# Several scheduling edits at once in an attention-and-expand kernel: opening order, value sums, value lag, and the start of the next product

## The chip, the cores and the metric

The kernel runs on one core of one Trainium2 chip. The metric is the device time of that core in microseconds, as the median of several executions. Experiments are compared with runs of the kernel before, made on the same chip in the same rounds.

## The reference

Hash attention feeds a gated expand and a contraction. Shapes: batch 4, 8 heads, 768 tokens, head width 64; the second half has 3072 tokens, width 512 and inner width 2048.

```python
q_bits = (einsum('bhsd,dk->bhsk', q, proj) > 0)      # 6 hash bits per token, the same for k
mask   = q_bucket[:, :, :, None] == k_bucket[:, :, None, :]
scores = where(mask, q @ k.T / sqrt(64), -1e9)
attn   = softmax(scores) ; x = attn @ v               # (B*S, H*D) = 3072 x 512
h = x @ w_in                                          # 512 -> 2048
s = sin(alpha * h)
out = (h + s * s / (alpha + 1e-9)) @ w_out            # 2048 -> 512
```

## The kernel before

The unit is a pair of heads: 16 pairs, four per batch. A pair takes 12 steps (2 heads x 6 key blocks). A step is two score matmuls, one exponential on ScalarE, and, some steps later, six value matmuls ("weigh"). After the first pair of each batch the batch before is expanded: 16 chunks F of 8 matmuls, sine, square and a close on VectorE. Its contraction (96 matmuls of 512 columns) is then mixed into the following pairs, two per step, by `fill`. Of the eight PSUM banks, six form three score slots of two; bank 6 and bank 7 take values and contraction sums.

```python
def weigh(step):                                     # values of one step
    if kb == 0:                                      # sum of all values, for empty buckets
        nc.tensor.matmul(out=regions..., lhsT=empty,
            rhs=vsum[:, hh, :]...broadcast [128, SB, D+1], start=True, stop=False)
    for qb in range(SB):
        nc.tensor.matmul(out=regions[...65 columns], lhsT=e[...], rhs=vaug[:, hh, kb, :],
                         start=False, ...)
    if kb == SB - 1:
        finish_head(i, hh, acc, xn)                  # VectorE: reciprocal, product

def attend(i, at_step, lag=2):
    accs = [banks[:, 6, :], banks[:, 7 if i <= NPAIR else 6, :]]
    for n in range(2 * SB):
        ...                                          # scores, exponential
        at_step(n)                                   # pieces of later pairs, loads, fill(2.0)
        while len(behind) > lag + (behind[0][2] == 0):
            weigh(behind.pop(0))

def prepare_on_pe(i):                                # pairs 0 to 5: hash bits on PE
    ...                                              # transposes on VectorE
    ps, held = slot(hold=True)                       # a score slot, held to the end
    hash_into(ps[:, 0], turned)                      # then pick into ps[:, 1]
    ...
    for h in range(2):
        if h == 1 and i == 0: give_back(held); ps, held = slot(hold=True)
        ...                                          # 12 transposes, two copies to aug
# [cut: prepare_by_dma for pairs 6 to 15 turns q and k by DMA transposes]

# expand:   h = banks[:, 6:8, :] if F % 4 == 2 else slot()[0]
# contract: o = banks[:, 7, :]; after 16 matmuls VectorE copies o to osb and it is stored
# at_step:  if n == 4: load(i + 3);  if n == 4 and 0 < i <= 4: weigh_in(...)  # one weight piece
```

The 16 weight pieces are 512 KB each, loaded as float32 and cast to bfloat16 on POOL; `weigh_in` issues one load and the cast of an earlier piece.

The softmax here doesn't subtract the row's maximum and nothing guards it: scores larger than these inputs give would overflow.

## Time and profile before

| | before |
|---|---|
| median | 334.79 us (3 runs, 334.19 to 336.34) |
| span of the profiled execution | 332.0 us |
| first exponential | 15.74 us |
| first expand begins, ends | 66.69, 87.69 us |
| last expand begins | 284.50 us |

The boundaries are start times of matmuls and exponentials in the trace. First the page's busy times (PE is TensorE's matmuls, PEld the loading of their stationary operand, DVE VectorE, ACT ScalarE, POOL GpSimd), then groups of it (busy us, mean ns of one, idle before and its releaser):

```profile
PE 305.9 (92%) x3016; PEld 184.5 (56%) x3041; DVE 182.2 (55%) x302; ACT 243.8 (73%) x299; POOL 93.8 (28%) x175
```

```profile
L367 ACT ACTIVATE e<-banks 128x768 bf16<-128x768 f32 x192 | 150.4, 810 | 42.4 <-PE banks L360 34.0
...
L333 PE MATMUL banks<-vsum,empty 128*128 128x390 bf16 x32 | 10.6, 331 | 0.0
```

The waits of PE (engine, line, what it waited for: total us, times, longest):

```profile
PE banks L427 <- DVE osb L435: 5.4, 15, 1.0
PE banks L427 <- DVE g L381: 5.2, 4, 1.9
PE banks L196 <- POOL w_hash L146: 4.4, 1, 4.4
PE banks L360 <- ACT e L367: 1.4, 5, 0.4
...
PE banks L427 <- POOL w_out_bf L175: 0.4, 1, 0.4
```

L427 is the contraction: it waits for the copy of its finished block (osb), and at its start for the expand's close (g) that still reads bank 7. L196 is the first hash. A busy PE of 92% includes pipeline tails; streaming times are smaller, so the prediction below counts them by hand.

Busy time by stretch (length, then busy us of PE, PEld, DVE, ACT, POOL; granted clock as a share of the full one; busy share of the DMA engines; GB/s). The first is attention alone, the second the first expand, the third a mixed stretch:

```profile
15.74:66.69 50.95, 48.91 (x812) 34.19 (x810) 31.56 (x66) 44.11 (x60) 25.45 (x48) 1.00 0.50 144
66.69:87.69 21.00, 21.00 (x145) 12.79 (x142) 18.24 (x24) 20.39 (x24) 9.23 (x9) 1.00 0.95 272
...
163.63:217.43 53.80, 50.38 (x534) 29.41 (x541) 25.02 (x48) 40.90 (x51) 11.25 (x21) 1.00 0.60 141
```

And four exponentials in a row, from the timeline (start, us, engine):

```profile
15.74 2.90 ACT L367 ACTIVATE e<-banks 128x768 bf16<-128x768 f32 x4
```

### The profile page before, as it was taken

Reading aid. Unit: us, or ns where it says so; the run is one execution under the profiler, and the core shown is the slowest. Engines: PE = TensorE matmul, PEld = TensorE weight load, DVE = VectorE, ACT = ScalarE, POOL = GpSimd, SP = SyncE. Lnnn points to the kernel's source line nnn. Section 1 sums busy time; section 2 is a strip of 40 time slices with the busy share of each in tenths; the row PEclk is TensorE's granted clock in tenths of the full one; section 3 lists DMA queues with packets and bytes.
Section 4 is the critical chain, followed back from the end, with each engine's and each line's share of the span. In section 5 each row is a group of like instructions: output and inputs, shape, how many; then the busy total and the mean of one; then the engine's idle time right before and its main releaser. Section 6 shows DMA issues by size and latency. Waiting matters only on the chain.

```text
span 332.0 us, 7598 instructions
## 1 busy us (share of the span) xinstructions
PE 305.9 (92%) x3016; PEld 184.5 (56%) x3041; DVE 182.2 (55%) x302; ACT 243.8 (73%) x299; POOL 93.8 (28%) x175
## 2 busy tenths in 40 slices
PE   4799999999889999999899999999899998998995
PEld 4566766666445555566455555566455554564442
DVE  3456566679943443559943443559943212499311
ACT  1287988999976777889987777889987776499000
POOL 2990256515779335235000235130000000000000
PEclk9699999999999999999999999999999999999999
DMA  7902767699874868963013958870015220200031
GB/s 240 331 2 51 206 210 231 169 204 330 299 256 82 222 88 231 218 137 118 0 42 60 237 116 211 216 114 0 3 38 77 85 55 16 72 2 0 11 117 64
DMA packets 68763, 42.86 MB, mean 129 GB/s; under 512 B 46728, under 2 KB 63608, under 8 KB 68728
## 3 DMA queue, kind: packets, MB, share of 16 engines
q1 hardware_dynamic: 68464, 42.37, 48.2%
q8 instruction: 24, 0.39, 0.5%
q14 instruction: 11, 0.09, 0.1%
q10 hardware_dynamic: 264, 0.01, 0.0%
HBM read 28.01 MB, written 7.27 MB: 106 GB/s over the span
## 4 chain that ended last, share of the span: by engine, by line
PE 77%; DMA 8%; DVE 6%; ACT 4%; issue 2%; SPq 2%; POOL 1%; ACTq 0%; POOLq 0%; DVEq 0%
PE banks L427 24%; PE banks L393 18%; PE banks L360 16%; PE banks L340 9%; PE banks L196 4%; DVE osb L435 3%; PE banks L251 3%; DMA w_1468<-in_moe_w_in_dram 3%; ACT e L367 2%; DMA w_1596<-in_moe_w_out_dram 2%; DMA proj_97<-in_proj_dram 2%; PE banks L333 2%; DMA w_1532<-in_moe_w_out_dram 1%; DVE g L381 1%; DMA ka<-kn 1%
## 5 line engine op out<-in xcount | busy, mean ns | idle before, releaser
L367 ACT ACTIVATE e<-banks 128x768 bf16<-128x768 f32 x192 | 150.4, 810 | 42.4 <-PE banks L360 34.0
L427 PE MATMUL banks<-w_out_bf,g 128*128 128x512 bf16 x359 | 98.9, 378 | 13.3 <-DVE osb L435 5.4
L360 PE MATMUL banks<-qa,ka 76*128 76x384 bf16 x384 | 93.1, 325 | 2.0 <-ACT e L367 1.4
L393 PE MATMUL banks<-xt,w_in_bf 128*128 128x384 bf16 x512 | 84.3, 326 | 0.0
L340 PEld LDWEIGHTS <-e 128*128 128x128 bf16 x1152 | 54.4, 97 | 30.4 <-issue 2.1
L393 PEld LDWEIGHTS <-w_in_bf 128*128 128x128 bf16 x512 | 49.7, 98 | 32.5
L427 PEld LDWEIGHTS <-g 128*128 128x128 bf16 x384 | 36.5, 97 | 48.4 <-issue 17.1
L402 ACT ACTIVATE s<-banks,alpha_sb 128x768 bf16<-128x768 f32 x64 | 57.1, 892 | 7.2 <-PE banks L393 5.9
L340 PE MATMUL banks<-vaug,e 128*128 128x65 bf16 x1152 | 60.6, 193 | 0.2 <-ACT e L367 0.2
L435 DVE COPY osb<-banks 128x512 f32<-128x512 f32 x24 | 16.6, 691 | 43.6 <-PE banks L427 43.6
L360 PEld LDWEIGHTS <-ka 76*128 76x128 bf16 x384 | 28.6, 98 | 11.9 <-issue 3.4
L315 DVE RECIPROCAL rden<-banks 128x6 f32<-128x6 f32 x32 | 6.1, 190 | 45.7 <-PE banks L340 45.7
L213 POOL TENSOR_TENSOR vacc<-vacc,vaug 128x130 f32<-128x130 f32 x48 | 20.3, 422 | 3.8
L281 DVE TENSOR_SCALAR bits<-banks,side 128x192 bf16<-128x192 f32 x20 | 7.4, 413 | 22.1 <-ACT e L367 11.5
L196 PE MATMUL banks<-qt,w_hash 128*32 128x192 f32 x128 | 14.3, 344 | 4.6 <-POOL w_hash L146 4.4
L316 DVE TENSOR_TENSOR xn<-banks,rden 128x384 bf16<-128x384 f32 x32 | 17.8, 558 | 1.1
L196 PE MATMUL banks<-kt,w_hash 128*32 128x192 f32 x128 | 14.3, 344 | 0.0
L196 PEld LDWEIGHTS banks<-qt,w_hash 128*32 128x32 f32 x128 | 6.5, 112 | 10.3 <-POOL w_hash L146 4.7
L251 PE MATMUL banks<-ident,nat 128*76 128x128 bf16 x144 | 11.1, 234 | 0.7 <-DVE nat L240 0.7
L251 PEld LDWEIGHTS <-nat 128*76 128x76 bf16 x144 | 10.3, 126 | 2.2 <-POOL vacc L210 0.8
L333 PE MATMUL banks<-vsum,empty 128*128 128x390 bf16 x32 | 10.6, 331 | 0.0
L255 ACT COPY ka<-banks 76x768 bf16<-76x768 bf16 x2 | 1.6, 794 | 12.0 <-PE banks L251 12.0
(269 smaller groups left out, 275.7 us busy)
## 6 DMA issues: line engine op xcount, KB each, us to landing
out_dram<-osb SPq DMA_DIRECT2D x24, 256.0 KB
rows<-bits SPq DMA_DIRECT2D x40, 24.0 KB
w_603<-in_moe_w_in_dram SPq DMA_DIRECT2D x1, 512.0 KB
w_823<-in_moe_w_in_dram SPq DMA_DIRECT2D x1, 512.0 KB
w_1048<-in_moe_w_in_dram SPq DMA_DIRECT2D x1, 512.0 KB
w_1270<-in_moe_w_in_dram SPq DMA_DIRECT2D x1, 512.0 KB
w_1421<-in_moe_w_in_dram SPq DMA_DIRECT2D x1, 512.0 KB
w_1436<-in_moe_w_in_dram SPq DMA_DIRECT2D x1, 512.0 KB
```

Of the source, the lines that this page charges most:

```text
L196: nc.tensor.matmul(out=ps[32 * j:32 * j + 32, 0:SB * 32].rearrange("p (s c) -> p s c", s=SB), lhsT=w_hash[:, blk].rearrange("p l a -> p (l ...
L213: nc.gpsimd.tensor_tensor(out=dst, in0=vacc[:, sb % 2], in1=vaug[:, :, sb], op=ALU.add)
L251: nc.tensor.transpose(out[:, s * 128:(s + 1) * 128], nat[:, s, 2 * t + h], ident)
L316: nc.vector.tensor_tensor(out=xn[:, :, hh, :], in0=cols[:, :, 0:D], in1=rden.unsqueeze(2).to_broadcast([128, SB, D]), op=ALU.mult,)
L333: nc.tensor.matmul(out=regions.rearrange("p (s e) -> p s e", e=D + 1), lhsT=empty, rhs=vsum[:, hh, :].unsqueeze(1).to_broadcast([128, SB, ...
L340: nc.tensor.matmul(out=regions[:, qb * (D + 1):(qb + 1) * (D + 1)], lhsT=e[:, qb * 128:(qb + 1) * 128], rhs=vaug[:, hh, kb, :], start=Fals ...
L360: nc.tensor.matmul(out=sc[:, half, 0:HALF], lhsT=ka[0:KA, hh, kb * 128:(kb + 1) * 128], rhs=qa[0:KA, hh, half * HALF:(half + 1) * HALF], s ...
L367: nc.scalar.activation(out=e.rearrange("p (h c) -> p h c", h=2), in_=sc[:, :, 0:HALF], func=AF.Exp, scale=SCALE,)
L393: nc.tensor.matmul(out=h[:, half, 0:HALF], lhsT=w_in_bf[:, p, F * 128:(F + 1) * 128], rhs=xt[b][:, p, half * HALF:(half + 1) * HALF], star ...
L402: nc.scalar.activation(out=s.rearrange("p (h c) -> p h c", h=2), in_=h[:, :, 0:HALF], func=AF.Sin, scale=alpha_sb[:, F:F + 1],)
L427: nc.tensor.matmul(out=o, lhsT=g[:, F, sub * 128:(sub + 1) * 128], rhs=w_out_bf[:, F, :], start=(F == 0), stop=(F == NF - 1),)
L435: nc.vector.tensor_copy(out=osb, in_=o)
```

## The change

Its intent is to take waits and work from PE: an earlier opening, score slots held for less time, value sums on VectorE for pairs 6 to 15, values three steps behind, a pause after a finished output block, and a contraction that begins inside the expand's last chunk. The diff, cut to its core:

```diff
+        nc.scalar.dma_start(out=proj_sb, in_=proj)            # one plain DMA, first
-            nc.scalar.dma_start(out=proj4[:, blk, :], in_=proj[...].to_broadcast([4, 32, NB]))
# w_hash copied half by VectorE, half by POOL; alpha prepared in the opening; 44 warm-up matmuls for 32
# prepare_on_pe: q and k turned in two pieces; hash and pick in bank 6 for i > 1
+        if i > 1: ps = banks[:, 6, :]
         for h in range(2):
-            if h == 1 and i == 0:
+            if held is not None:
                 give_back(held)
-                ps, held = slot(hold=True)
+            ps, held = slot(hold=True)
# prepare_by_dma: base = the value sums of a pair, one 130-column matmul, copied to SBUF
# finish_head, i >= 6:  total = acc + base  on VectorE, then reciprocal and product
-        if kb == 0:
+        if kb == 0 and not apart:                             # apart = i >= ON_PE
-    def attend(i, at_step, lag=2):
+    def attend(i, at_step, lag=3):
-            while len(behind) > lag + (behind[0][2] == 0):
+            while len(behind) > lag:
# expand
+            at_chunk(F, g)                # last chunk: queue the contraction and fill(4.0, 4)
-            h = banks[:, 6:8, :] if F % 4 == 2 else slot()[0]
+            h = banks[:, 6:8, :] if F in (3, 7, 11) else slot()[0]
# straight after the expand fill(8.0, 8); before, two steps' scores came first
# fill: at most three a step, and none in the step after a finished block ("rest")
# the last output block goes out in two column halves
-            at = [(i - 2, 6 + late), (i - 2, 10 + late // 2), (i - 1, 0), (i - 1, 2), (i - 1, 4), (i - 1, 6)]
+            at = [(i - 2, n) for n in (4, 7, 11)] + [(i - 1, n) for n in (1, 2, 3, 5, 6, 6, 8)]
-                if n == 4 and i + 3 < n_pairs:
+                if n == 6 and i + 3 < n_pairs:
                     load(i + 3)
-                if n == 4 and 0 < i <= NPAIR:
+                if n == 7 and 0 < i <= NPAIR:
                     weigh_in(1 if i < NPAIR else 0)
```

More of the change, by code (lines that the diff above doesn't have):

```diff
@@ L47 @@
     KA = D + 2 * NB
+    ON_PE = 6
     SCALE = 1.0 / (D ** 0.5)
@@ L95, in load @@
                 loaded[i, name] = t
-    proj4 = const.tile([128, 2, NB], FP32, name="proj4")
+    proj_sb = const.tile([D, NB], FP32, name="proj_sb")
     w_hash = const.tile([128, 2, 8, 4], FP32, name="w_hash")
@@ L118, in hash_constants @@
         nc.vector.memset(empty, EMPTY)
-        for blk in range(2):
-            nc.scalar.dma_start(
-                out=proj4[:, blk, :],
-                in_=proj[32 * blk:32 * blk + 32, :].unsqueeze(0).to_broadcast([4, 32, NB]),
-            )
         nc.vector.memset(w_hash, 0.0)
@@ L145, in hash_constants, with invert_alpha @@
         for a in range(4):
-            nc.gpsimd.tensor_copy(
-                out=w_hash[32 * a:32 * a + 32, :, 0:NB, a], in_=proj4[32 * a:32 * a + 32])
+            for blk, engine in ((0, nc.vector), (1, nc.gpsimd)):
+                engine.tensor_copy(
+                    out=w_hash[32 * a:32 * a + 32, blk, 0:NB, a],
+                    in_=proj_sb[32 * blk:32 * blk + 32, :])
     def load_alpha():
-        nc.sync.dma_start(out=alpha_raw, in_=moe_alpha.rearrange("(F p) -> F p", p=128))
+        nc.scalar.dma_start(out=alpha_raw, in_=moe_alpha.rearrange("(F p) -> F p", p=128))
+    def invert_alpha():
         nc.vector.tensor_copy(out=ident32, in_=ident[0:NF, 0:NF])
-    def invert_alpha():
         nc.tensor.transpose(banks[:, 7, 512 - NF:512], alpha_raw, ident32)
@@ L179, with turn_blocks @@
     operands = {}
-    def turn_blocks(i):
-        q2, k2 = loaded.pop((i, "q")), loaded.pop((i, "k"))
-        turned = []
-        for name, src in (("q", q2), ("k", k2)):
-            t = hash_pool.tile([128, 2, SB, 2, 32], FP32, name=f"{name}t")
-            nc.vector.transpose(
-                out=t.rearrange("p h s b c -> p (h s b c)"),
-                in_=src.rearrange("p h s d -> p (h s d)"),
-            )
-            turned.append(t)
-        return q2, k2, turned
+    def turn_blocks(name, src):
+        t = hash_pool.tile([128, 2, SB, 2, 32], FP32, name=f"{name}t")
+        nc.vector.transpose(
+            out=t.rearrange("p h s b c -> p (h s b c)"),
+            in_=src.rearrange("p h s d -> p (h s d)"),
+        )
+        return t
     def hash_into(ps, turned):
-        for j in range(4):
-            for blk in range(2):
+        for blk in range(2):
+            for j in range(4):
                 nc.tensor.matmul(
@@ L216, in prepare_on_pe @@
     def prepare_on_pe(i):
-        q2, k2, turned = turn_blocks(i)
+        q2, k2 = loaded.pop((i, "q")), loaded.pop((i, "k"))
+        turned = [turn_blocks("q", q2)]
         nat = hash_pool.tile([128, SB, 4, KA], BF16, name="nat")
@@ L224, in prepare_on_pe @@
         yield
-        ps, held = slot(hold=True)
-        hash_into(ps[:, 0], turned)
+        turned.append(turn_blocks("k", k2))
+        yield
+        held = None
+        if i > 1:
+            ps = banks[:, 6, :]
+        else:
+            ps, held = slot(hold=True)
+            ps = ps[:, 0, :]
+        hash_into(ps, turned)
         bits = hash_pool.tile([128, SB, 32], BF16, name="bit")
         nc.vector.tensor_scalar(
-            out=bits.rearrange("p s c -> p (s c)"), in0=ps[:, 0, 0:SB * 32],
+            out=bits.rearrange("p s c -> p (s c)"), in0=ps[:, 0:SB * 32],
             scalar1=bound[:, 0:1], scalar2=None, op0=ALU.is_gt,
@@ L232, in prepare_on_pe @@
         yield
-        picked = ps[:, 1, 0:SB * 8 * NB].rearrange("p (s m) -> p s m", s=SB)
+        picked = ps[:, SB * 32:SB * (32 + 8 * NB)].rearrange("p (s m) -> p s m", s=SB)
         for s in range(SB):
@@ L244, in prepare_on_pe @@
         for h in range(2):
-            if h == 1 and i == 0:
+            if held is not None:
                 give_back(held)
-                ps, held = slot(hold=True)
+            ps, held = slot(hold=True)
             for t in range(2):
@@ L251, in prepare_on_pe @@
                     nc.tensor.transpose(out[:, s * 128:(s + 1) * 128], nat[:, s, 2 * t + h], ident)
-            for t in range(2):
-                out = ps[0:KA, t, 0:HALF].bitcast(BF16)
-                if i == 0 and t == 1:
+                if (i, h, t) == (0, 0, 1):
                     nc.scalar.copy(out=aug[t][0:KA, h, :], in_=out)
@@ L257, in prepare_on_pe @@
                     nc.vector.tensor_copy(out=aug[t][0:KA, h, :], in_=out)
-            yield
+                yield
+        values = take_values(i)
+        operands[i] = (*aug, *values)
+        yield
         give_back(held)
-        operands[i] = (*aug, *take_values(i))
     def prepare_by_dma(i):
-        q2, k2, turned = turn_blocks(i)
+        vaug, vsum = take_values(i)
+        yield
+        q2, k2 = loaded.pop((i, "q")), loaded.pop((i, "k"))
+        turned = [turn_blocks("q", q2), turn_blocks("k", k2)]
         nats = []
@@ L290, in prepare_by_dma @@
             )
+        base = v_pool.tile([128, 2, D + 1], FP32, name="base")
+        room = ps[:, 1, 0:2 * (D + 1)]
+        nc.tensor.matmul(
+            out=room, lhsT=empty, rhs=vsum.rearrange("p h e -> p (h e)"), start=True, stop=True)
+        nc.vector.tensor_copy(out=base.rearrange("p h e -> p (h e)"), in_=room)
         yield
@@ L303, in prepare_by_dma @@
                 )
-        yield
-        operands[i] = (*aug, *take_values(i))
+        operands[i] = (*aug, vaug, vsum, base)
     xt = {}
@@ L314, in finish_head @@
         cols = acc[:, 0:SB * (D + 1)].rearrange("p (s e) -> p s e", e=D + 1)
+        if i >= ON_PE:
+            total = x_pool.tile([128, SB, D + 1], FP32, name="total")
+            nc.vector.tensor_tensor(
+                out=total, in0=cols,
+                in1=operands[i][4][:, hh].unsqueeze(1).to_broadcast([128, SB, D + 1]), op=ALU.add,
+            )
+            cols = total
         nc.vector.reciprocal(out=rden, in_=cols[:, :, D])
@@ L329, in weigh @@
         i, hh, kb, e, acc, xn = step
-        _, _, vaug, vsum = operands[i]
+        vaug, vsum = operands[i][2:4]
         regions = acc[:, 0:SB * (D + 1)]
-        if kb == 0:
+        apart = i >= ON_PE
+        if kb == 0 and not apart:
             nc.tensor.matmul(
@@ L343, in weigh @@
                 rhs=vaug[:, hh, kb, :],
-                start=False, stop=(kb == SB - 1 and qb == SB - 1),
+                start=(apart and kb == 0 and qb == 0), stop=(kb == SB - 1 and qb == SB - 1),
             )
@@ L352, in attend @@
             xt[b] = xt_pool.tile([128, NPAIR, S], BF16, name="xt")
-        qa, ka, vaug, vsum = operands[i]
+        qa, ka = operands[i][0:2]
         accs = [banks[:, 6, :], banks[:, 7 if i <= NPAIR else 6, :]]
@@ L372, in attend, with expand @@
             at_step(n)
-            while len(behind) > lag + (behind[0][2] == 0):
+            while len(behind) > lag:
                 weigh(behind.pop(0))
-    def expand(b, at_step):
+    def expand(b, at_chunk):
         g = g_pool.tile([128, NF, S], BF16, name="g")
@@ L411, in expand @@
             close(F, s2, h)
-            at_step(F)
-        return g
     rows_of = [out[b * S:(b + 1) * S, :].rearrange("(p s) d -> p s d", s=SB) for b in range(B)]
@@ L420, in contract @@
         last = b == B - 1
-        order = [(sub, F) for sub in range(SB) for F in range(NF)]
+        order = [(sub, F, 0, DMODEL) for sub in range(SB) for F in range(NF)]
         if last:
-            order[:2 * NF] = [(sub, F) for part in (range(12), range(12, NF))
+            order[:2 * NF] = [(sub, F, 0, DMODEL) for part in (range(12), range(12, NF))
                               for sub in range(2) for F in part]
-        for sub, F in order:
-            o = banks[:, 7 - (sub % 2 if last else 0), :]
+            order[-NF:] = [(SB - 1, F, c, c + DMODEL // 2) for c in (0, DMODEL // 2)
+                           for F in range(NF)]
+        for sub, F, c0, c1 in order:
+            o = banks[:, 7 - ((sub + (c0 > 0)) % 2 if last else 0), c0:c1]
             nc.tensor.matmul(
@@ L429, in contract @@
                 lhsT=g[:, F, sub * 128:(sub + 1) * 128],
-                rhs=w_out_bf[:, F, :],
+                rhs=w_out_bf[:, F, c0:c1],
                 start=(F == 0), stop=(F == NF - 1),
@@ L434, in contract @@
                 osb = o_pool.tile([128, DMODEL], FP32, name="osb")
-                nc.vector.tensor_copy(out=osb, in_=o)
-                nc.sync.dma_start(out=rows_of[b][:, sub, :], in_=osb)
+                nc.vector.tensor_copy(out=osb[:, c0:c1], in_=o)
+                nc.sync.dma_start(out=rows_of[b][:, sub, c0:c1], in_=osb[:, c0:c1])
             yield F == NF - 1
@@ L442, with fill @@
     owed = 0.0
-    def fill(rate):
-        nonlocal owed
+    rest = False
+    def fill(rate, most=3):
+        nonlocal owed, rest
         owed += rate
-        while owed >= 1.0 and todo:
+        if rest:
+            rest = False
+            return
+        while owed >= 1.0 and todo and most:
             owed -= 1.0
+            most -= 1
             done = next(todo[0], None)
@@ L452, in fill @@
             if done:
+                rest = True
                 break
     def drain():
-        nonlocal owed
+        nonlocal owed, rest
         while todo:
             fill(1.0)
-        owed = 0.0
+        owed, rest = 0.0, False
     IN_ATTEND = 2.0
     n_pairs = len(pairs)
-    ON_PE = 6
     parts = {}
@@ L468 @@
         if i == 1:
-            at = [None, (0, 3), (0, 4), (0, 5), (0, 7), (0, 9)]
+            at = [(0, n) for n in (1, 2, 4, 5, 7, 8, 8, 10)]
         elif i < ON_PE:
-            late = 2 if i == 2 else 0
-            at = [(i - 2, 6 + late), (i - 2, 10 + late // 2), (i - 1, 0), (i - 1, 2), (i - 1, 4), (i - 1, 6)]
-        else:
-            at = [(i - 2, 6), (i - 2, 10), (i - 2, 11), (i - 1, 3), (i - 1, 5), (i - 1, 6)]
-        for part in at[1:] if i == 1 else at:
+            at = [(i - 2, n) for n in (4, 7, 11)] + [(i - 1, n) for n in (1, 2, 3, 5, 6, 6, 8)]
+        else:
+            at = [(i - 2, n) for n in (3, 6, 10, 11)] + [(i - 1, n) for n in (1, 3)]
+        for part in at:
             parts.setdefault(part, []).append(i)
@@ L480 @@
         hash_constants()
+        load_alpha()
         load(0, "kv")
         load(1, "qk")
-        for _ in range(32):
+        for _ in range(44):
             nc.tensor.matmul(out=banks[:, 7, 0:128], lhsT=empty, rhs=empty, start=True, stop=True)
-        for _ in prepare_on_pe(0):
-            pass
         load(1, "v")
         load(2)
+        first = prepare_on_pe(0)
+        for _ in range(3):
+            next(first)
+        invert_alpha()
+        for _ in range(3):
+            next(first)
         under_way = {1: prepare_on_pe(1)}
-        next(under_way[1])
+        for _ in range(2):
+            next(under_way[1])
+        for _ in first:
+            pass
         weights = iter(range(16))
@@ L499, in weigh_in, with at_chunk @@
                 cast_w(*held_w.popleft(), nc.gpsimd)
+        done = 0
+        def at_chunk(F, g):
+            nonlocal done
+            if done == 0:
+                weigh_in(2)
+            if F == NF - 1:
+                todo.append(contract(done, g))
+                done += 1
+                fill(4.0, 4)
         for i in range(n_pairs):
@@ L508, in at_step @@
                     next(under_way[p], None)
-                if (i, n) == (1, 4):
-                    load_alpha()
-                if (i, n) == (3, 4):
-                    invert_alpha()
-                if n == 4 and i + 3 < n_pairs:
+                if n == 6 and i + 3 < n_pairs:
                     load(i + 3)
-                if n == 4 and 0 < i <= NPAIR:
+                if n == 7 and 0 < i <= NPAIR:
                     weigh_in(1 if i < NPAIR else 0)
-                if n == 0 and i % NPAIR == 1:
-                    return
                 fill(IN_ATTEND)
@@ L523 @@
                 drain()
-                g = expand(b - 1, lambda F: weigh_in(2) if b == 1 else None)
-                todo.append(contract(b - 1, g))
-                owed = 8.0
+                expand(b - 1, at_chunk)
+                fill(8.0, 8)
         while behind:
@@ L529 @@
         drain()
-        todo.append(contract(B - 1, expand(B - 1, lambda F: None)))
+        expand(B - 1, at_chunk)
         drain()
```

## The prediction

> **What bounds it now.** TensorE. The page gives PE 92% busy, but that counts pipeline tails. From the timeline, streaming rates are 0.1625 us per 384-column matmul (120 in 19.50 us), 0.2155 us per 512-column one, 0.03 us per 65-column value matmul (six between starts 0.18 us apart), 0.81 us per hash group of 16, 0.33 us per pick group, 0.67 us per 12 transposes. Summed over the counts this is about 291 us of the 332 us span. The Trainium skill, "TensorE: Matmul & The Clock Gate" (Part 1), says N/2.4 GHz + 2.5 ns; the 0.1625 us agrees. So about 41 us are gaps, tails and the cold start.
>
> Stages by windows: opening 0 to 14.7; five attention pairs alone 14.7 to 68 (53 us; ScalarE's 60 exponentials of 0.81 us are a floor of 48.6 us); four expands of 21 us, in which PE, ACT and DVE are all near 100%; three stretches of attention with the contraction mixed in (54, 54, 46 us; per step PE 0.94 us against ACT 0.81, so PE-bound); last contraction 21 us.
>
> **What the change does, costed.**
> 1. Opening. The waits view shows the first hash waiting 4.4 us for w_hash, whose projection DMA landed at 8.0 us. One plain DMA issued first should land near 3 us, so the hash waits for the transpose of k (ends 7.1) instead: 2 us. PE idle shrinks from 4.4 us to about 2, so the clock may stay up (0.57 was granted in 8 to 16 us; hash group 1.6 us there, 0.81 later). First scores from 14.8 to about 12: -2.5 to -3.
> 2. Attention alone: hash no longer holds a score slot, lag three: ACT idle there is about 3 to 4 us, I give back -1.5.
> 3. Start of contraction. PE waited 1.1, 1.1, 1.0, 1.9 us for bank 7, which chunk 14 of the expand held. Now chunks 3, 7, 11 hold it, and four matmuls run inside the last chunk: about -4.5.
> 4. Pause after a finished output block: waits for the osb copy, 5.4 us in 15 pieces (up to 1.0): -4.
> 5. Value sums: 20 matmuls of 390 columns (0.165 us) go, ten of 130 columns (about 0.06) come: -2.7 on PE. DVE gets 20 adds of about 0.56 us and ten small copies, off the path since DVE is near 50% there. But both heads use bank 6, and the next head's values now come one step (about 0.76 us) after the last, while the add frees the bank after about 0.8: 0.1 to 0.2 us stall a head, +2 to +3.
> 6. Last output in halves: -0.4.
> 7. First contraction reaches the last w_out chunk sooner; its DMAs are already back to back (about 0.95 share, cast ended 95.5): +1.
>
> Sum: about -14 to -16 us.
>
> **Predicted: 319.5 us, 80% range 313 to 327.** Chances: faster by over 2% 0.89, within 2% 0.09, slower 0.02.
>
> **What would show it.** First scores near 12 us and no long hash wait; the waits for osb and g on the contraction nearly gone from the waits view; the value-sum group down from 32 to 12; PE idle in the mixed stretches down, each about 4 us shorter; expands unchanged at 21 us plus 0.9 for the four matmuls; a new wait of the value matmuls on the DVE add, small and about 20 times; a wait on the w_out cast in the first contraction.
>
> **What would make it wrong.** The add delayed behind DVE transposes or copies, so that bank 6 is freed late and PE stalls more than 3 us; the hash in bank 6 held by value matmuls, or too few score slots in the first pairs; w_out arriving so late that stage one loses its gain; or the idle being shifted to ScalarE's floor instead of vanishing.

## More of the kernel before

Nearly all DMAs are issued from SP's queue, in program order.

## The result, and the profile after

The changed kernel took 325.48 us (median of 4 runs, 324.83 to 327.25) against 335.21 us (4 runs) for the kernel before. The ratio is 0.9717, 95% interval 0.9666 to 0.9769. A ratio is the mean time of one kernel's fast runs over that of the other's of the same rounds, so it isn't quite the ratio of the medians. The gain is inside the predicted range but below its middle: 9.7 us, not 15.

The same stretches from the two traces show where it came from (us, start to start):

| stretch | before | after | difference |
|---|---|---|---|
| start to first exponential | 15.74 | 13.69 | -2.05 |
| to the first expand (attention alone) | 50.95 | 53.45 | **+2.50** |
| first expand and pair 5, to the first exponential of pair 6 | 38.21 | 40.63 | **+2.42** |
| from there to the last expand | 179.60 | 170.20 | -9.40 |
| last expand to the end | 47.51 | 45.98 | -1.53 |
| span | 332.01 | 323.95 | -8.06 |

The first 108 us of the changed kernel are slower than before by 2.9 us, and all the gain lies behind them. The lines that answer to those of before:

```profile
PE 305.0 (94%) x3059; PEld 183.3 (57%) x3059; DVE 196.7 (61%) x338; ACT 242.9 (75%) x298; POOL 94.6 (29%) x175
```

```profile
L387 ACT ACTIVATE e<-banks 128x768 bf16<-128x768 f32 x192 | 149.9, 810 | 36.7 <-PE banks L380 29.4
...
L328 DVE TENSOR_TENSOR total<-banks,base 128x390 f32<-128x390 f32 x20 | 11.2, 561 | 36.8 <-PE banks L360 36.7
...
L353 PE MATMUL banks<-vsum,empty 128*128 128x390 bf16 x12 | 4.0, 331 | 0.1
```

PE's waits after the change:

```profile
PE banks L255 <- ACT e L387: 2.4, 6, 0.4
PE banks L360 <- DVE total L328: 1.9, 2, 0.9
PE banks L449 <- POOL w_out_bf L174: 1.5, 3, 0.7
PE banks L380 <- ACT e L387: 1.4, 6, 0.4
PE banks L414 <- POOL w_in_bf L174: 1.2, 2, 0.7
...
PE banks L414 <- DMA xt<-xn: 0.9, 1, 0.9
...
PE banks L449 <- DVE osb L457: 0.2, 1, 0.2
```

The waits for osb fell from 5.4 to 0.2 us, those of the contraction for g are gone, and the first hash's wait for w_hash is gone. There are new ones: transposes of the hash preparation (L255) behind exponentials, and the weights (w_in, w_out). By stretch:

```profile
13.69:67.14 53.45, 49.36 (x807) 33.35 (x806) 30.79 (x62) 44.54 (x59) 28.19 (x55) 1.00 0.43 127
67.14:90.77 23.63, 22.40 (x155) 13.21 (x152) 19.87 (x26) 20.94 (x24) 10.39 (x10) 1.00 1.07 307
...
165.26:215.36 50.10, 48.60 (x529) 28.07 (x528) 29.17 (x58) 40.13 (x50) 13.53 (x27) 1.00 0.63 147
```

In the third of these PE is busy 97% (48.60 of 50.10), up from 94%: the mixed stretch is close to PE's own work.

Inside one pair of attention alone (pair 2, from the timeline):

```profile
39.38 1.51 ACT L387 ACTIVATE e<-banks 128x768 bf16<-128x768 f32 x2 [0.20 <-PE banks L380]
...
40.24 0.49 PE L255 MATMUL banks<-ident,nat 128*76 128x128 bf16 x6 [0.45 <-ACT e L387]
...
40.94 0.48 PE L380 MATMUL banks<-qa,ka 76*128 76x384 bf16 x2
...
41.52 4.51 ACT L387 ACTIVATE e<-banks 128x768 bf16<-128x768 f32 x6 [0.63 <-PE banks L380]
```

The second head's transposes stand in front of the next scores in PE's order and wait 0.45 us for an exponential. ScalarE then idles 0.63 us. In each of these pairs the same pattern returns: 10.62 us between the first exponentials of pairs 1, 2, 3 and 4, against 9.95, 9.94 and 10.22 before.

### The profile page after: what moved, and what is told of

Same layout as the page of the kernel before. It is cut to its first block, busy times and chain, and to the rows that moved or that the text cites. A ratio compares the mean times of both kernels' runs of the same rounds, so it can differ in the third digit from the quotient of the medians.

```text
span 323.9 us, 7681 instructions
## 1 busy us (share of the span) xinstructions
PE 305.0 (94%) x3059; PEld 183.3 (57%) x3059; DVE 196.7 (61%) x338; ACT 242.9 (75%) x298; POOL 94.6 (29%) x175
## 4 chain that ended last, share of the span: by engine, by line
PE 66%; DMA 12%; DVE 6%; ACT 5%; POOL 5%; SPq 4%; issue 2%; ACTq 0%; DVEq 0%; POOLq 0%
PE banks L414 21%; PE banks L449 19%; PE banks L380 12%; PE banks L360 7%; ACT e L387 4%; PE banks L191 3%; PE banks L255 2%; DMA v_3064<-in_v_dram 2%; DMA k_150<-in_k_dram 2%; DMA v_3276<-in_v_dram 2%; SPq L92 2%; SPq L279 2%; DMA w_1467<-in_moe_w_in_dram 2%; DMA v_1090<-in_v_dram 1%; DMA w_1611<-in_moe_w_out_dram 1%
## 5 line engine op out<-in xcount | busy, mean ns | idle before, releaser
L449 PE MATMUL banks<-w_out_bf,g 128*128 128x512 bf16 (+1 forms) x400 | 102.1, 370 | 1.9 <-POOL w_out_bf L174 1.5
L360 PEld LDWEIGHTS <-e 128*128 128x128 bf16 x1152 | 57.6, 97 | 35.4 <-issue 6.7
L360 PE MATMUL banks<-vaug,e 128*128 128x65 bf16 x1152 | 64.9, 193 | 2.0 <-DVE total L328 1.9
L449 PEld LDWEIGHTS <-g 128*128 128x128 bf16 x400 | 38.7, 97 | 35.5 <-issue 3.7
L457 DVE COPY osb<-banks 128x512 f32<-128x512 f32 (+1 forms) x25 | 16.7, 668 | 30.4 <-PE banks L449 30.4
L328 DVE TENSOR_TENSOR total<-banks,base 128x390 f32<-128x390 f32 x20 | 11.2, 561 | 36.8 <-PE banks L360 36.7
L380 PEld LDWEIGHTS <-ka 76*128 76x128 bf16 x384 | 26.9, 99 | 6.1 <-issue 3.1
L255 PE MATMUL banks<-ident,nat 128*76 128x128 bf16 x144 | 12.5, 231 | 4.2 <-ACT e L387 2.4
L255 PEld LDWEIGHTS <-nat 128*76 128x76 bf16 x144 | 11.0, 123 | 8.6 <-issue 3.7
L334 DVE TENSOR_TENSOR xn<-total,rden 128x384 bf16<-128x384 f32 x20 | 11.9, 597 | 0.7
L259 DVE COPY qa<-banks 76x768 bf16<-76x768 bf16 x12 | 6.6, 550 | 8.7 <-PE banks L255 8.7
L232 DVE TENSOR_SCALAR bit<-banks,bound 128x192 bf16<-128x192 f32 x6 | 2.5, 418 | 8.5 <-PE banks L191 8.5
```

The lines of the kernel that those rows point to most:

```text
L255: nc.tensor.transpose(out[:, s * 128:(s + 1) * 128], nat[:, s, 2 * t + h], ident)
L328: nc.vector.tensor_tensor(out=total, in0=cols, in1=operands[i][4][:, hh].unsqueeze(1).to_broadcast([128, SB, D + 1]), op=ALU.add,)
L334: nc.vector.tensor_tensor(out=xn[:, :, hh, :], in0=cols[:, :, 0:D], in1=rden.unsqueeze(2).to_broadcast([128, SB, D]), op=ALU.mult,)
L360: nc.tensor.matmul(out=regions[:, qb * (D + 1):(qb + 1) * (D + 1)], lhsT=e[:, qb * 128:(qb + 1) * 128], rhs=vaug[:, hh, kb, :], start=(apa ...
L380: nc.tensor.matmul(out=sc[:, half, 0:HALF], lhsT=ka[0:KA, hh, kb * 128:(kb + 1) * 128], rhs=qa[0:KA, hh, half * HALF:(half + 1) * HALF], s ...
L449: nc.tensor.matmul(out=o, lhsT=g[:, F, sub * 128:(sub + 1) * 128], rhs=w_out_bf[:, F, c0:c1], start=(F == 0), stop=(F == NF - 1),)
```

## The experiments

"Changed" below is the changed kernel. All twelve gave correct results. None was timed in the same rounds as the changed kernel itself, so their ratios to the kernel before are compared with its 0.9717, and single stretches are read from the traces. "Mixed part" is the time from pair 6's first exponential to the last expand: 179.60 us before, 170.20 after.

| run | median us | ratio to before | pairs 2, 3 (us each) | first expand | mixed part |
|---|---|---|---|---|---|
| changed | 325.48 | 0.9717 | 10.62 | 23.63 | 170.20 |
| e1_hold | 324.18 | 0.9705 | 9.92 | 26.40 | 170.66 |
| e2_pick | 326.28 | 0.9760 | 10.39 | 25.58 | 170.12 |
| e3_load4 | 332.56 | 0.9956 | 10.62 | 22.16 | 177.19 |
| e4_three | 329.79 | 0.9876 | 9.69 | 23.23 | 178.04 |
| e5_sum_pe | 331.58 | 0.9896 | 10.62 | 25.11 | 175.83 |
| e6_norest | 329.74 | 0.9848 | 10.62 | 24.95 | 173.61 |
| e7_lag2 | 324.34 | 0.9697 | 10.78 | 22.94 | 169.35 |
| e8_nochunk | 328.21 | 0.9802 | 10.62 | 24.92 | 171.24 |
| e9_bank | 333.96 | 0.9974 | 10.62 | 23.56 | 174.53 |
| e11_sum_lag2 | 327.15 | 0.9755 | 10.78 | 24.17 | 173.04 |
| e12_weights | 328.18 | 0.9807 | 10.62 | 23.47 | 170.44 |
| e13_joint | 327.41 | 0.9752 | 9.69 | 23.49 | 171.95 |

The medians are of all timed executions. Of e5_sum_pe, e8_nochunk and e13_joint one execution was slow; the ratios leave it out. The 95% intervals of the ratios are about 0.004 to 0.009 to either side, so e1_hold, e2_pick, e7_lag2, e11_sum_lag2, e12_weights and e13_joint aren't told from the changed kernel by their times, and e8_nochunk only just.

The column of the first expand has a noise of its own. e6_norest runs the program of the changed kernel up to the first finished output block, yet its first expand took 24.95 us against 23.63. It began 1.33 us earlier, after a luckier opening, and ended at the same time (90.76 and 90.77 us).

### Why attention alone got slower: e1_hold, e2_pick

My theory: the change exchanges the score slot between a pair's two heads, and the oldest slot is one that an exponential still reads. The rival: the pair is bound by PE's work or by the later place of hash and pick.

```diff
# e1_hold
-            if held is not None:
-                give_back(held)
-            ps, held = slot(hold=True)
+            if h == 0 or i <= 1:
+                if held is not None:
+                    give_back(held)
+                ps, held = slot(hold=True)
```

> The changed kernel, but from the third pair on the score slot taken for a pair's first head is kept for its second head instead of being given back and exchanged for the oldest slot. Theory (slot exchange): in the changed kernel the second head's transposes wait for the exponential that still reads the exchanged slot (0.45 us in each of pairs 1 to 4, and the next exponential comes 1.44 us after the one before instead of 0.7). Kept, this wait goes: pairs 1 to 4 fall from 10.62 us each to about 10.1, total -2 us (about 323.5). Rival (the pair is bound by the amount of PE work, or by the later place of pick): pairs stay at 10.6 and the total at 325.5.

The pairs fell to 9.92 us, a little more than expected, so the exchanged slot is shown as the cost: 0.70 us a pair. The total did not follow. The first expand began 3.8 us earlier (1.5 us of it from the opening) and grew to 26.40 us, so that it ended only 1.0 us earlier. The granted clock was 1.00 throughout it, and PE waited for weights:

```profile
PE banks L415 <- POOL w_in_bf L174: 3.1, 2, 2.6
```

```diff
# e2_pick
-            at = [(i - 2, n) for n in (4, 7, 11)] + [(i - 1, n) for n in (1, 2, 3, 5, 6, 6, 8)]
+            at = [(i - 2, n) for n in (4, 7, 10)] + [(i - 1, n) for n in (0, 2, 3, 5, 6, 6, 8)]
```

> The changed kernel, but hash and pick of pairs 2 to 5 stand one step earlier (steps 10 and 0, as before the change). Theory (pick too close to the transposes): the transposes of the first half wait for the DVE copy of the picked bits, and the gap between exponentials 2 and 3 of a pair is 1.16 us instead of 0.71; with the step back it falls to about 0.8, pairs 1 to 4 fall by about 0.3 us each, total about -1 us. Rival (only the slot exchange costs): the gap moves to another step and the pairs stay at 10.6.

The pairs fell by 0.23 us to 10.39, near the expected 0.3. In total nothing was gained: the first expand again took up the time (25.58 us). So two causes are shown for the pairs, 0.70 and 0.23 us, and together they give the 9.69 us of e4_three and e13_joint. With both removed, attention alone takes 50.14 us in e13_joint, against 53.45 with the change and 50.95 before it.

### The first expand: e3_load4, e4_three, e12_weights, e13_joint

The fourth weight piece is w_1270 before the change and w_1341 after it. SP's queue, before:

```profile
62.12 0.46 SPq L171 DMA_DIRECT2D w_1270<-in_moe_w_in_dram  x1
62.69 1.36 SPq L272 DMA_TRANSPOSE qa<-qn  x1
64.15 3.75 SPq L272 DMA_TRANSPOSE ka<-kn  x1
```

and after:

```profile
64.58 1.21 SPq L279 DMA_TRANSPOSE qa<-qn  x1
65.89 1.23 SPq L279 DMA_TRANSPOSE ka<-kn  x1
...
68.81 0.47 SPq L170 DMA_DIRECT2D w_1341<-in_moe_w_in_dram  x1
```

The piece moved from step 4 to step 7 in the program, which put it behind the transposes of pair 6 in the queue; those wait for POOL. Step numbers are an order in a queue, not a time.

```diff
# e3_load4
-                if n == 6 and i + 3 < n_pairs:
+                if n == 4 and i + 3 < n_pairs:
-                if n == 7 and 0 < i <= NPAIR:
+                if n == 4 and 0 < i <= NPAIR:
```

> The changed kernel, but the loads of q, k, v and of a weight stand at step 4 again instead of 6 and 7. Theory (late fourth weight): in the changed kernel that DMA was issued at 68.8 us behind the transposes of pair 6 in the queue's order (62.1 before the change), so the first expand waits 1.2 us for w_in and the first contraction 1.5 us for w_out; with step 4 the w_in wait goes, the first expand falls from 23.6 to about 22.2 us, total -1.5 us. Rival (the weights are bound by DMA bandwidth once the expand has begun): the w_out waits stay or grow by what w_in loses, and the total moves by less than 0.5 us.

The first half of the theory held: no wait for w_in is left, and the first expand took 22.16 us. The waits for w_out grew to 2.9 us, as the rival said, and first expand and pair 5 together took 40.60 us, as in the changed kernel (40.63). But the total was missed by far: 332.56 us, 7 us slower than the changed kernel. Pair 11 took 17.12 us instead of 12.19. The timeline of e3_load4 there:

```profile
188.05 0.40 SPq L92 DMA_DIRECT2D q<-in_q_dram  x1
...
190.09 1.34 SPq L279 DMA_TRANSPOSE qa<-qn  x1
...
196.98 0.35 DVE L307 COPY qa<-qa 64x768 bf16<-64x768 bf16 x1 [4.31 <-DMA qa<-qn]
...
198.53 0.68 DVE L457 COPY osb<-banks 128x512 f32<-128x512 f32 x1
...
199.26 0.81 PE L449 MATMUL banks<-w_out_bf,g 128*128 128x512 bf16 x3 [3.21 <-DVE osb L457]
```

The loads of q, k and v (three of 384 KB) now went out just ahead of the transposes of the next pair. These landed late; VectorE, which works in order, waited 4.31 us for them at L307; the finished output block waited behind it, and PE 3.21 us for that. Such waits total 4.8 us in this run, against 0.2 in the changed kernel. The clock was also granted at half from 200.5 to 203.9 us, which is part of the loss. So the later loads at step 6, which I had passed over, protect the mixed stretches: by some 7 us there, in which no weights are loaded any more. What was delayed at the first expand is the weight piece, which is the other of the two lines. Loads at step 6 with the weight at step 4 were not run.

> All three edits together. If the three causes are separate the gains add: about -4 to -4.5 us against the changed kernel, about 321 us; pairs 1 to 4 near 9.9 us each, first expand near 22.2 us. If they share one limit (PE work of about 8.9 us and an exponential cadence of 0.70 us a step leave room, so I do not expect it) the sum is less than its parts.

e4_three is e1_hold, e2_pick and e3_load4 together. The pairs reached 9.69 us, and the first expand took 23.23 us; the mixed part paid for the early loads again (178.04 us). Its first pair also ran at half clock: 15.18 us, with a granted clock of 0.50 from 12 to 20 us. The gains don't add.

```diff
# e12_weights: two pieces a pair, loads of q, k, v left at step 6
-                if n == 7 and 0 < i <= NPAIR:
-                    weigh_in(1 if i < NPAIR else 0)
+                if n in (7, 9) and 0 < i <= NPAIR:
+                    weigh_in(1)
```

> The changed kernel with two weight pieces per pair in pairs 1 to 4 (steps 7 and 9) instead of one, so that eight instead of twelve remain for the first expand. Theory (the end of the first expand and the first contraction are gated by the weights' DMA): waits on w_in and w_out vanish, the first expand falls from 23.6 to about 22.1 us, about 2.5 us in all, total about 323. Rival (something else gates them, or the added early DMA delays q, k, v as loads at step 4 did): no gain, or pairs 2 to 4 longer than 10.62.

The w_in wait went, but the w_out wait stayed (2.1 us) and the expand took 23.47 us. With a third fewer pieces left, the last cast still ended near 96 us. The queue says why:

```profile
59.92 1.22 SPq L339 DMA_TRANSPOSE xt<-xn  x1
67.33 1.21 SPq L279 DMA_TRANSPOSE qa<-qn  x1
68.65 1.23 SPq L279 DMA_TRANSPOSE ka<-kn  x1
```

SP issued nothing between 61.2 and 67.3 us, and the weight loads of pair 4 and all later ones stood behind the transposes that it issued then. Over 65 to 70 us the DMA share was 0.22; then it was above 0.85 until 90 us. The clock fell as well (the windows view of e12_weights):

```profile
90.00:95.00 5.00, 2.90 (x14) 1.21 (x13) 3.16 (x5) 3.83 (x4) 3.49 (x5) 1.00 0.73 247
95.00:100.00 5.00, 4.83 (x22) 2.08 (x22) 2.53 (x3) 2.32 (x3) 4.61 (x9) 0.66 0.17 60
```

After five microseconds in which PE was busy for 2.90, the next five were granted 0.66 of the clock, and pair 5 took 15.57 us instead of 13.56. That the waits caused the drop is not shown. In e6_norest PE was busy for even less at this point, and the clock stayed at 1.00, in this stretch and after it:

```profile
91.95:96.95 5.00, 2.43 (x10) 0.96 (x10) 2.44 (x4) 3.01 (x4) 3.93 (x4) 1.00 0.66 253
```

> Kept score slot, hash and pick one step earlier, and the earlier weights, together. Theory (the gain in pairs 1 to 4 was swallowed by the wait for weights): pairs 1 to 4 near 9.7 us as in the run with all three, and now the first expand stays near 22.1 us, so the 3.5 us of the pairs and the 2.5 us of the weights add: total about 320. Rival (another gate behind the weights): 323 or more.

e13_joint joins e1_hold, e2_pick and e12_weights. Its first expand ended at 86.60 us, 4.2 us before that of the changed kernel, and pair 6 began at 107.92 us, 0.15 us after it.

```profile
PE banks L450 <- POOL w_out_bf L174: 4.2, 5, 1.3
```

The head start went to two things: waits for the weights of the contraction, and the clock, which was granted at half from 92.1 to 98.9 us. All traces together tell the two apart. Here are the casts of the last weight piece in the changed kernel, in e6_norest and in e13_joint:

```profile
94.74 1.09 POOL L174 CAST w_out_bf<-w_1611 128x1024 bf16<-128x1024 f32 x1 [0.29 <-DMA w_1611<-in_moe_w_out_dram]
...
96.17 1.04 POOL L174 CAST w_out_bf<-w 128x1024 bf16<-128x1024 f32 x1 [0.20 <-DMA w<-in_moe_w_out_dram]
...
92.58 1.04 POOL L174 CAST w_out_bf<-w 128x1024 bf16<-128x1024 f32 x1 [0.23 <-DMA w<-in_moe_w_out_dram]
```

In the changed kernel and the ten experiments with the full clock here, the first exponential of pair 6 came 11.8 to 12.5 us after the end of this cast, though the first expand began anywhere from 63.4 to 67.4 us. In e12_weights and e13_joint, with 3.4 and 6.8 us at half clock, it came 13.3 and 14.3 us after it. So up to pair 6 the kernel keeps the pace of the last weight piece, and on this count about 2 of e13_joint's 4.2 us went to the weights (their last cast ended only 2.2 us earlier) and the rest, an estimate, to the clock. The theory that two weights a pair lift this gate fell. That it would go if weights were issued from another queue wasn't tried and stays open.

### The mixed stretches: e5_sum_pe, e7_lag2, e11_sum_lag2

```diff
# e5_sum_pe: no base, no add; apart = False
-        if i >= ON_PE:
+        if False:
-        apart = i >= ON_PE
+        apart = False
# e7_lag2
-    def attend(i, at_step, lag=3):
+    def attend(i, at_step, lag=2):
-            while len(behind) > lag:
+            while len(behind) > lag + (behind[0][2] == 0):
# e11_sum_lag2: both
```

> The changed kernel with the value sums of all pairs on PE again (20 more matmuls of 390 columns, no add on DVE, no base). Theory (mixed stretches are PE-bound, 0.165 us each): +3.3 us less the DVE-add stalls of about 1.9 us and less ten small matmuls, so +1 to +2 us against the changed kernel; the mixed pairs grow by about 0.2 us each. Rival (the moved sums are off the path): no change within 0.5 us, or even faster if the add's stalls cost more than the waits view shows.

> The changed kernel with the values two steps behind (three for a head's first block), the rule before the change. Theory: with two steps the next head's first value block comes two steps after the last of the head before, so the stalls on the DVE add (1.9 us in total) go, but values wait more for exponentials: within 1 us either way. Rival (the lag of three is what costs 0.67 us a pair in pairs 1 to 4, since it moved the values against the transposes): those pairs fall to about 10 us.

> The changed kernel with the value sums on PE (as in the run that lost 6 us) and in addition the old rule of two steps (three for a head's first block). Theory (interaction): with a lag of three the sum matmul follows the head before by one step only and waits for DVE's reciprocal and product in the same bank; the old rule gives it two steps. Then each pair of the mixed stretches costs only the streaming 0.33 us more than in the changed kernel instead of 0.57, and the total is about 328 (against 331.6 with lag three). Rival (the sums cost 0.57 us a pair in themselves): total 331 to 332.

The mixed part of the four combinations:

| | value sums on PE | sums on VectorE |
|---|---|---|
| two steps (three for a head's first block) | 173.04 (e11_sum_lag2) | 169.35 (e7_lag2) |
| three steps | 175.83 (e5_sum_pe) | 170.20 (changed) |

Under the old rule the moved sums are worth 3.7 us of the mixed part, near the 20 x 0.165 = 3.3 us of streaming that they take from PE there (ten pairs of two heads). Under the lag of three they are worth 5.6. So the two edits belong together: three steps with the sums on PE costs 2.8 us, because a head's first matmul then follows the head before by one step. The trace shows it: a head's sum matmul started 0.49 to 0.50 us after the matmul before it for 13 of the 20 heads in e5_sum_pe, but 0.21 to 0.27 us after it for 18 of them in e11_sum_lag2. Over all heads that is 3.5 us more. The waits view lists only the longest two of these waits in either run. e5_sum_pe was expected to lose 1 to 2 us and lost 6.1, which I had underestimated for this reason; e11_sum_lag2 was expected at 328 and came at 327.15. The lag of three by itself brings nothing here: e7_lag2 took 324.34 us. As the rival for attention alone it is refuted, since pairs 2 and 3 took 10.78 us under the old rule.

### The pause and the start of the contraction: e6_norest, e8_nochunk, e9_bank

```diff
# e6_norest
-                rest = True
+                rest = False
```

> The changed kernel without the pause after a finished output block. Theory: the waits of the contraction for the osb copy come back, about 15 of 0.3 to 0.4 us, +4 to +5 us against the changed kernel, all in the mixed stretches. Rival (PE time is conserved by something else there): less than 2 us.

It lost 4.3 us in total, 3.4 of it in the mixed part, and the waits for osb were back. The pause is confirmed.

```profile
PE banks L449 <- DVE osb L457: 3.9, 10, 0.8
```

```diff
# e8_nochunk
-                fill(4.0, 4)
...
-                fill(8.0, 8)
+                fill(12.0, 12)
# e9_bank: as e8_nochunk, and
-            h = banks[:, 6:8, :] if F in (3, 7, 11) else slot()[0]
+            h = banks[:, 6:8, :] if F % 4 == 2 else slot()[0]
```

> The changed kernel with no contraction matmuls inside the last chunk of the expand: twelve after it instead of four in it and eight after. The bank choice (chunks 3, 7, 11) stays. Theory: the bank choice is what removed the waits of 1.1, 1.1, 1.0 and 1.9 us, and the four matmuls inside the chunk only moved; the middle transitions change by less than 0.3 us each, and expand plus first exponential keep their sum. In the last contraction a wait on g does not return since 24 matmuls need none of the last chunk. Total within 1 us of the changed kernel, perhaps faster as the sine of the last chunk starts 0.86 us sooner. Rival (the early start is the gain): +2 to +4 us.

> The changed kernel with both parts of the new contraction start undone: no matmuls inside the last chunk, and the expand's chunks 2, 6, 10, 14 in the value banks again. Theory from the run without the early start (which kept expands of 22 us against 21 before the change): the bank choice itself slows each expand by about 1.05 us, because its last chunks have only three slots, and gains back the 1.1 us wait for bank 7; so here the expands return to 21.0 to 21.1 us, waits on g of about 1.1 us (1.9 at the end) return before the contraction, and the total equals that of the run without the early start (328.2) within 1 us. Rival (what I predicted: the bank choice is worth 4.5 us): total 331 to 333.

Without the early start the kernel took 328.21 us, 2.7 us more than the changed one (2.4 by the medians of the fast executions), so my theory that the four matmuls only moved is wrong. Its second and third expand kept their length (21.99 and 22.43 us against 22.12 and 22.05), and PE waited for g in the last chunks:

```profile
PE banks L414 <- DVE g L401: 3.6, 4, 1.5
```

With three slots at the end, the last chunk must wait for a close, and the four contraction matmuls (0.86 us) fit into that hole. In the stretches after the expands, e8_nochunk lost 0.58 us in pair 9 and in pair 13 each, and 0.86 us in the last contraction.

In e9_bank the expands were back at 21.2 and 21.3 us, and the contraction waited for bank 7:

```profile
PE banks L449 <- DVE g L401: 7.8, 4, 2.1
```

It took 333.96 us; my theory (no difference from e8_nochunk) fell and the rival stands. But e9_bank puts twelve matmuls straight behind the expand, ahead of the scores of the next pair, whose first exponential came 5.34 us after the expand instead of 3.45. The kernel before had the scores of two steps between. So 5.8 us is what the bank choice is worth in the new order, and not what it alone would have brought to the kernel before.

## Why the prediction was right or wrong

The range and the verdict were right; the middle was 6 us too low. A part of that is luck: attention alone was missed by 4 us, and the later stretches gave more than was counted. Point by point:

1. **Opening: right in kind, the size goes with the clock.** -2.05 us in the profiled run, -2.5 to -3 predicted. Among the experiments, whose opening is unchanged, the first exponential came at 11.78 to 13.63 us. In the profile of the changed kernel the clock did fall (0.83 in 8 to 12 us, 0.74 in 12 to 16); in e6_norest it stayed at 1.00 and the first exponential came at 11.78. The four traces of this opening without a fall lie at 11.78 to 12.16 us, the nine with one at 12.62 to 13.69.
2. **"Attention alone: hash no longer holds a score slot ... I give back -1.5": wrong, +2.50 us.** This is the step that failed. The hash left its slot, but the heads now exchange theirs, and the transposes wait for the exponential in it (0.70 us a pair, e1_hold), and pick stands too close to its transposes (0.23 us, e2_pick). I had read that the slot is held for fewer steps and not asked which slot comes next. The floor was wrong as well: I took 0.81 us per exponential for the cadence, while four in a row take 2.90 us: they overlap, and start (2.90 - 0.81) / 3 = 0.70 us apart. The Trainium skill, "ScalarE: Activation LUTs" (What ACT_TABLE_LOAD costs), has it: "Back-to-back ACTIVATEs overlap by ≈ 93 ns." The trace shows 0.11 us (0.81 - 0.70).
3. **Start of the contraction, -4.5: right in kind.** The waits for g went. The price is expands (the second to the fourth) of 22.05 to 22.60 us, which with 0.86 us of contraction in them is 0.2 to 0.7 us more than I had said.
4. **Pause, -4: right.** 5.4 us of waits became 0.2; e6_norest lost 4.3 us.
5. **Value sums, -2.7 and +2 to +3 of stalls: the gain right, the stalls right in sum and wrong in kind.** The waits view shows only two stalls of the values on the add (1.9 us), and 2.0 us in two pieces with the old rule as well, so the lag didn't make them. Small ones exist below what that view lists: for twelve heads the first value matmul started 0.05 us after the end of the add and 0.27 us after the contraction matmul before it, which streams in 0.215. That is 0.06 us each, 0.7 in all, and not 0.1 to 0.2 for each of twenty.
6. **First contraction (item 7), +1: the sign right, the size too small.** The first expand and pair 5 cost +2.42 us. I had looked at w_out alone; the moved line held back a w_in piece as well. But that isn't the reason: e3_load4 put it back, and the stretch still took 40.60 us. What fits the traces is that the contraction asks for w_out sooner (first matmul at 88.77 us, before 90.16) and stands with eight matmuls in front of the next scores, while the last piece is cast no sooner (95.83 us, before 95.53). PE waited 1.5 us for w_out instead of 0.4. That this makes up the 2.42 us is argued; a later start of the first contraction alone was not run.
7. **The sum was wrong in arithmetic.** Points 1 to 7 as written add to -2.75 - 1.5 - 4.5 - 4 - 2.7 + 2.5 - 0.4 + 1 = -12.35, while the text says -14 to -16. Added rightly, the middle would have been 322.4 us. What is left, 3 us, is less than the error of point 2 alone (4 us, from -1.5 to +2.50); from pair 6 on the kernel did better than I said, -10.93 us against -9.1 for the prediction's items 3 to 6, a part of which falls before pair 6.

The fate of the early gain matters most. In e13_joint 4.2 us won before the end of the first expand are gone by pair 6, by the estimate above about half of them to the clock. In e1_hold, at full clock, 2.8 us of a head start of 3.8 were gone at the end of the first expand. Up to pair 6 the kernel runs at the pace of the weights.

## What to carry to other kernels

Before you shorten a stage, find out what its end is waiting for: here most of what was gained before the first expand ran into weights that came little sooner. Where one queue issues nearly everything, moving an issue by two steps is a change of order among waits, so it should be read, and tried, as closely as a moved matmul. And when you hand a buffer back and take another, ask who still reads the one you get.

## What the Trainium skill lacked or had wrong

- "DMA: Bandwidth & Descriptors" (Issuing engines are not separate DMA queues) says that issuing from several engines "will only save the time on the sequencer it takes to initiate the DMA". That section doesn't speak of loads held behind an issue that waits for data in the same queue: here SP issued nothing from 61.2 to 67.3 us (e12_weights), with the DMA share at 0.22 from 65 to 70 us, while weights were needed. Whether a second queue would have helped was not run.
- "TensorE: Matmul & The Clock Gate" (Part 1) ties the drop of the clock to an idle window of about 3.4 us; its section on "A second HAM failure mode" names frequent short idling, without a number. In e12_weights no wait of PE in the stretch was longer than 1.29 us; a stretch of 5 us with PE busy for 2.90 was followed by one at a mean clock of 0.66, and pair 5, in which it fell, took 2 us longer than in the changed kernel. Nor does the busy share of such a stretch decide it: e6_norest had 2.43 us in 5 and kept the clock at 1.00. What does is left open.
- No lack, but checked here: the same page's K/N of 4/8 when cold agrees with the 0.50 granted from 12 to 20 us in e4_three, and its N / 2.4 GHz + 2.5 ns with the 0.1625 us of a 384-column matmul. It says that warm-up depends on a free-running window; here the same opening, with 44 warm-up matmuls, gave first exponentials between 11.78 and 13.69 us.
